# Clustered attention and a mixing MLP on one core: weighted values of a head pair in one run instead of two, with a new table of places

## The chip, the cores and the metric

The kernel runs on one core of a Trainium2 chip. The metric is the time of one execution on the device in microseconds. Before the change it is 1022.99 us, the median of two runs (1021.92 and 1024.06). One more execution was profiled.

## The reference

Attention over 4 batches, 8 heads, 768 positions and 64 dimensions, in which a query sees only keys of its own cluster, and after it a mixing layer and a multilayer stage, all in float32:

```
q_assign, k_assign = argmax over 16 centroids of the cosine with q and with k
mask    = q_assign[:, :, :, None] == k_assign[:, :, None, :]
scores  = where(mask, (q @ k.T) / 8, -1e9);  scores -= max(scores)
attn    = exp(scores) / (sum(exp(scores)) + 1e-9)
x       = (attn @ v), heads side by side                  # (4, 768, 512)
u       = x + ((x.T @ U) @ V).T                           # U: 768x32, V: 32x768
out     = u + relu(u @ w_ch1) @ w_ch2                     # 512 -> 2048 -> 512
```

## The kernel before, in words

**Stages.** Two heads are worked on together as a pair; there are 16 pairs, i = 0 to 15, four to a batch. After the attention of all pairs comes the multilayer stage (`gemm1`, `gemm2`, lines 600 to 624), which the change leaves alone.

**A pair.** `load` (L329) and `load_v` (L335) fetch queries and keys, and values, on the DMA queue of SyncE (SP). `sims` (L339) multiplies them with the centroids: four products into the four 32-column strips of the array, so narrow products. `largest` (L348) transposes the result, and DVE takes its maximum; `clusters` (L361) makes one-hot rows out of it, in place, in the same bank of PSUM. `clusters_T` and `place_clusters` bring these beside the keys, so that one product gives score and mask at once. `split_hi` (ACT) and `split_lo` (L390; DVE for one half, POOL for the other) make a high and a low part of queries and keys, and `place_keys_hi`, `place_keys_lo`, `place_queries`, `place_ones` copy parts of them on SP. `rowmax` (L445) makes a first score, 24 steps of one product and one reduction on DVE per pair; `rowmax_T` and `rowmax_place` bring the maxima back in as a row, by a DMA on ACT's queue. `scores` (L471) is run for 2 halves (h) times 6 blocks of keys (c): four products into one of two PSUM tiles `st`, and one exponential on ACT into a tile `pr`, of which there are 11. `weights` (L485) adds the exponentials of a half into a tile `T` (three buffers), mostly on POOL, five adds per half. `values` (L494) multiplies exponentials with values: per step two float32 products, one into the upper and one into the lower 64 columns of the array, each of them two instructions in the trace; six steps accumulate into one bank, which ACT then empties. `sums` (L506) multiplies the two T of a pair with a column of ones, four narrow products; `sums_T` and `normalise` finish the pair. After each batch `mix_u`, `mix_sum` and `mix_v` do the mixing layer.

All small PSUM tiles (`ps_max`, `ps_sim`, `ps_simT`, `o_ps`, `ps_sum`, ...) share the four work banks of `work` (L139). The weights of the multilayer stage arrive as float64 bits in between, joined to float32 by DVE and split in two parts by ACT and POOL (`load_weights`, L189).

**Order.** Each call is put on a list with a time (`at`, L639) and the list is sorted (L733); `keep_order` (L107) then keeps every engine to the order of the list. The times are in slots, 12 to a pair: `when(name, i)` is 12i plus an entry of the table `times` (L59), whose columns stand for kinds of pairs ("most", "last of a batch", "last", "first", "second", "third"). So each engine takes its instructions strictly in this order, and waits where one isn't ready.

The lines of the loop (L693 to L699) that place scores, values and adds; `GV` is 6, so values come in batches of six steps, 24 products as the trace counts them:

```
for k in range(NS):
    h, c = divmod(k, NT)
    at(when("scores", i) + k, scores, i, h, c)
    at(when("values", i) + GV * (k // GV) + GV - 1 + 0.001 * (k % GV), values, i, h, c)
    if c:
        at(when("weights", i) + k, weights, i, h, c)
at(when("sums", i), sums, i)
```

`GV` also groups the places of `rowmax` (L685), by the list `spots`.

Of the kernel before, what the change touches and what calls it, by code (L numbers as in the profile page):

```python
# [29 lines left out]
F32 = mybir.dt.float32  # L30
# [23 lines left out]
GV = 6  # L54
# [8 lines left out]
    "clusters_T":      (-19.46, -19.14,  -17.8,   None, -12.09, -13.37),  # L63
    "place_clusters":  (-18.22, -16.28, -15.03,   None, -10.34, -12.11),
    "split_hi0":       (-29.17, -30.74, -24.29,   None,   None, -21.38),
    "split_lo0":       (-24.05, -24.44, -24.04,   None,   None, -18.43),
    "split_hi1":       (-23.81, -23.71, -24.34,   None,   None, -19.53),
    "split_lo1":       (-23.67, -20.02, -23.57,   None,   None, -17.17),
    "place_keys_hi":   (-20.09, -23.61, -22.66,   None,   None, -17.07),
    "place_keys_lo":   (-19.84, -19.85,  -21.7,   None,   None, -16.87),  # L70
    "place_queries":   (-16.97, -16.19,  -16.3,   None,   None, -16.28),
    "place_ones":      (-14.55, -12.25,  -6.11,   None,   None, -20.84),
# [8 lines left out]
    "sums_T":          ( 16.16,  15.81,   14.3,  15.86,  17.06,  16.44),  # L81
    "normalise0":      ( 18.83,  16.88,  14.88,  19.57,  20.85,  21.01),
# [4 lines left out]


mixes = {
    "mix_u":    ( 18.88,  18.35,  18.48,  16.57),  # L90
    "mix_sum":  ( 19.11,   19.1,  19.15,  18.35),
    "mix_v":    (  20.5,   20.4,  20.68,  19.42),
}
# [671 lines left out]
```

## Time and profile before

| | |
|---|---|
| median of two runs | 1022.99 us |
| profiled execution, its own time | 1020.33 us |
| its span, first to last instruction | 1018.5 us |
| mean granted clock of TensorE | 0.993 |
| busy PE, DVE, POOL, ACT over the span | 97, 48, 35, 34% |
| first and last `values` product begin at | 42.1 and 461.0 us |

Engines are called PE (TensorE), DVE (VectorE), ACT (ScalarE), POOL (GpSimd) and SP (SyncE). A row of the timeline gives start and length in us, engine, line, operation, what it writes and reads, shape, and how many instructions were merged; in brackets the idle time of the engine before it and who ended it. Lengths of products overlap, so their pace is read from the starts. A row of groups gives the count behind x, then busy us and mean ns of one, and then the idle time before them. A row of stretches gives the length and the busy time of PE, weight loads, DVE, ACT and POOL, the granted clock, the share of DMA and GB/s.

### The profile page before, as it was taken

To read this page: it belongs to the slowest core of one execution; us is meant where nothing else is said; L and a number is where in the kernel's file an instruction comes from. 1 tells how busy PE (TensorE), PEld (TensorE's weight loads), DVE (VectorE), ACT (ScalarE), POOL (GpSimd) and SP (SyncE) were. 2 spreads that over 40 slices of the span, in tenths; PEclk is the share of its full clock that TensorE was granted. 3 is DMA by queue.
4 is the path that set the end of the run, shared out by engine and by line. 5 is a ranking of instruction groups with operands and counts; after the bars stand their busy time and mean duration, and the time that the engine had idled before them with its cause. 6 is when DMAs were issued, how large, how long until landed. Compare 5 with 4: busy or idle time off the path is not lost.

```text
span 1018.5 us, 13723 instructions
## 1 busy us (share of the span) xinstructions
PE 990.5 (97%) x5368; PEld 786.9 (77%) x5368; DVE 490.5 (48%) x914; ACT 347.7 (34%) x572; POOL 359.4 (35%) x246
## 2 busy tenths in 40 slices
PE   5899999999999999989999999999999999999998
PEld 3566666676667666657899999999999999998997
DVE  5797777777777666768772121121221211212211
ACT  4454554555556554564341111111111111111110
POOL 5466676888788967753230000000000000000000
PEclk9899999999999999999999999999999999999999
DMA  7754554656465636243431001010010010100000
GB/s 186 191 130 115 157 146 122 192 155 156 100 199 136 150 86 181 61 143 108 163 123 63 1 32 32 1 62 1 1 63 1 18 46 1 62 1 1 32 1 32
DMA packets 28687, 87.71 MB, mean 86 GB/s; under 512 B 4880, under 2 KB 9488, under 8 KB 28112
## 3 DMA queue, kind: packets, MB, share of 16 engines
q1 hardware_dynamic: 28240, 86.76, 30.5%
q8 instruction: 42, 0.69, 0.3%
q14 instruction: 21, 0.17, 0.1%
q10 hardware_dynamic: 384, 0.10, 0.0%
HBM read 42.99 MB, written 12.58 MB: 55 GB/s over the span
## 4 chain that ended last, share of the span: by engine, by line
PE 90%; DVE 5%; ACT 1%; issue 1%; POOL 1%; DMA 1%; ACTq 0%; SPq 0%; POOLq 0%; DVEq 0%
PE o_ps L500 12%; PE ps_h L606 9%; PE ps_h L608 9%; PE ps_h L607 9%; PE y L624 9%; PE y L623 9%; PE y L622 9%; PE ps_max L453 7%; PE st L477 6%; PE st L479 6%; DVE m L455 2%; PE ps_sum L512 1%; PE ps_sim L343 1%; PE ps_oT L533 1%; PE ps_uT L595 1%
## 5 line engine op out<-in xcount | busy, mean ns | idle before, releaser
L492 POOL TENSOR_TENSOR T<-T,pr 128x768 f32<-128x768 f32 x120 | 226.5, 1887 | 44.9 <-ACT pr L482 19.3
L612 DVE SCALAR_TENSOR_TENSOR hl<-ps_h,hh 128x384 fp32r<-128x384 f32 x128 | 71.2, 556 | 349.9 <-ACT hh L611 349.8
L455 DVE TENSOR_REDUCE m<-ps_max 128x1 f32<-128x384 f32 x384 | 195.2, 547 | 80.6 <-PE ps_max L453 79.0
L611 ACT ACTIVATE hh<-ps_h 128x384 fp32r<-128x384 f32 x128 | 62.9, 491 | 373.8 <-PE ps_h L608 373.8
L482 ACT ACTIVATE pr<-st 128x768 f32<-128x768 f32 x192 | 154.3, 812 | 83.5 <-PE st L479 65.4
L453 PE MATMUL ps_max<-arena 128*128 128x384 f32 x384 | 126.6, 380 | 6.9 <-DVE oh L369 2.5
L500 PE MATMUL o_ps<-pr,vt 128*64 128x384 f32 x768 | 132.2, 494 | 0.1
L623 PE MATMUL y<-w2l,hh 128*128 128x512 f32 x288 | 113.6, 395 | 0.0
L477 PE MATMUL st<-arena 128*128 128x384 f32 x384 | 104.9, 354 | 2.0 <-ACT pr L482 2.0
L453 PEld LDWEIGHTS ps_max<-arena 128*128 128x128 f32 x384 | 70.5, 192 | 45.4 <-issue 21.4
L500 PEld LDWEIGHTS o_ps<-pr,vt 128*64 128x64 f32 x768 | 52.7, 138 | 66.4 <-issue 59.8
L479 PE MATMUL st<-arena 97*128 97x384 f32 x384 | 99.2, 340 | 2.8 <-DMA arena<-mT 2.8
L477 PEld LDWEIGHTS st<-arena 128*128 128x128 f32 x384 | 66.2, 190 | 17.9 <-issue 9.3
L492 POOL TENSOR_TENSOR T<-pr 128x768 f32<-128x768 f32 x30 | 56.6, 1886 | 62.2 <-ACT pr L482 62.2
L624 PE MATMUL y<-w2h,hl 128*128 128x512 f32 x192 | 76.1, 396 | 0.0
L624 PE MATMUL y<-arena,hl 128*128 128x512 f32 x192 | 76.0, 396 | 0.0
L622 PE MATMUL y<-w2h,hh 128*128 128x512 f32 x192 | 75.1, 391 | 0.0
L622 PE MATMUL y<-arena,hh 128*128 128x512 f32 x192 | 74.8, 390 | 0.0
L479 PEld LDWEIGHTS st<-arena 97*128 97x128 f32 x384 | 70.4, 190 | 3.5 <-issue 2.2
L623 PEld LDWEIGHTS y<-w2l,hh 128*128 128x128 f32 x288 | 54.0, 188 | 9.1
L504 ACT COPY os<-o_ps 128x384 f32<-128x384 f32 x32 | 15.3, 480 | 104.7 <-PE o_ps L500 104.7
L606 PE MATMUL ps_h<-arena,w1h 128*128 128x384 f32 x128 | 44.8, 350 | 0.2 <-DVE arena L598 0.2
(132 smaller groups left out, 1597.3 us busy)
## 6 DMA issues: line engine op xcount, KB each, us to landing
rw<-in_w SPq DMA_DIRECT2D x32, 512.0 KB
R<-in_qk SPq DMA_DIRECT2D x32, 384.0 KB
arena<-arena SPq DMA_DIRECT2D x32, 384.0 KB
arena<-arena SPq DMA_DIRECT2D x64, 192.0 KB
vt<-in_v SPq DMA_DIRECT2D x16, 384.0 KB
u_scr<-xt SPq DMA_DIRECT2D x4, 1536.0 KB
u<-u_scr SPq DMA_DIRECT2D x8, 768.0 KB
out_y<-u SPq DMA_DIRECT2D x24, 256.0 KB
```

What stands on the lines that cost most here:

```text
L453: nc.tensor.matmul(ps[:, 0:HS], x1[:, 0, g // 2, g % 2, t * P:(t + 1) * P], x1[:, 1, h, g % 2, :], start=True, stop=True)
L455: nc.vector.reduce_max(live["m2", i][:, h, u:u + 1], ps[:, 0:HS], axis=AX.X)
L477: nc.tensor.matmul(st[:, j, 0:HS], x1[:, 1, hk, j, ks], x1[:, 0, h, j, :], start=True, stop=False)
L479: nc.tensor.matmul(st[:, j, 0:HS], x2[0:97, 1, hk, j, ks], x2[0:97, 0, h, j, :], start=False, stop=True)
L482: nc.scalar.activation(pr, st[:, :, 0:HS], AF.Exp, scale=SCALE)
L492: eng.tensor_add(T, live["p", i, h, 0] if c == 1 else T, live["p", i, h, c])
L500: nc.tensor.matmul(o_ps[64 * j:64 * j + 64, 0:HS], vv[:, c, j, :], pr[:, j, :], start=(c == 0), stop=(c == NT - 1))
L606: nc.tensor.matmul(ps[:, 0:HS], w1h[:, d, fs], uh[:, d, :], start=(d == 0), stop=False)
L607: nc.tensor.matmul(ps[:, 0:HS], w1h[:, d, fs], ul[:, d, :], start=False, stop=False)
L622: nc.tensor.matmul(y[t], hh[:, ts], w2h[:, f % FG, :], start=(f == 0), stop=False)
L623: nc.tensor.matmul(y[t], hh[:, ts], w2l[:, f % FG, :], start=False, stop=False)
L624: nc.tensor.matmul(y[t], hl[:, ts], w2h[:, f % FG, :], start=False, stop=(f == NF - 1))
```

## The change

`GV` becomes 12 and a new `GM` = 6 keeps the grouping of `rowmax`. So all 12 steps of a pair's values stand together, 48 products by the trace's count, and `sums` gets its place from them, half a slot after the last. `sims` of pair i now stands straight ahead of the values of pair i - 4, and `largest` of pair i straight ahead of the values of pair i - 3, wherever there is such a pair. There are 13 `pr` buffers instead of 11, two `vt` (values) instead of three, two `T` instead of three. Nearly all entries of `times`, `mixes`, `stages` and `spots` are new. No instruction is added or taken away.

Around the run of pair 6 the sorted list reads before (left) and after (right):

```
before, first half of the pair's values        after
  72.31  values (5, 1, 0..5)                     84.00  scores (7, 0, 0)
  ...                                            84.12  rowmax (8, 3, 1)
  78.31  values (6, 0, 0..5)                     84.41  split_lo (9, 0)
  ...                                            84.45  largest (9)
  84.12  rowmax (8, 3, 1)                        84.46  sims (10)
  84.31  values (6, 1, 0..5)                     84.47  values (6, 0..1, 0..5)
  84.61  rowmax (8, 4, 0)                        84.61  rowmax (8, 4, 0)
  84.95  largest (9)                             84.97  sums (6)
  86.31  sums (6)                                85.00  scores (7, 0, 1)
  86.70  clusters (9)                            85.60  clusters (9)
  94.90  sims (10)                               86.07  sums_T (6)
```

The diff, with the tables cut to the entries that the prediction speaks of:

```diff
--- before.py
+++ after.py
@@ -51,57 +51,58 @@
 NF = DF // P
 NG = 4
 FG = NF // NG
-GV = 6
+GV = 12
+GM = 6
 BIG = float(2.0 ** 60)
 SCALE = 0.125
 
 
 times = {
-    "load0":           (-34.78, -34.39, -43.85,   None,   None, -25.08),
-    "load1":           (-26.29, -29.07, -32.88,   None,   None, -24.23),
-    "sims":            ( -25.1, -28.59, -28.41,   None,   None, -21.52),
...
-    "place_clusters":  (-18.22, -16.28, -15.03,   None, -10.34, -12.11),
...
-    "split_lo0":       (-24.05, -24.44, -24.04,   None,   None, -18.43),
...
-    "load_v":          ( -19.2,  -5.08,  -7.21,   None, -22.04,  -9.26),
+    "load0":           ( -40.5,  -40.5,  -40.5,   None,   None,    -27),
+    "load1":           (-38.82,    -39, -38.79,   None,   None,  -25.5),
+    "sims":            (-24.38, -28.52, -28.41,   None,   None,  -24.5),
...
+    "place_clusters":  (-19.29,  -18.3,  -18.3,   None, -10.11, -13.71),
...
+    "split_lo0":       (-23.59, -24.44, -24.04,   None,   None, -20.27),
...
+    "load_v":          ( -8.39,  -8.42,   -8.5,   None,   -8.5,  -8.19),
...
-    "rowmax_T":        ( -3.08,  -3.31,  -3.73,  -3.18,   0.25,  -2.19),
-    "rowmax_place":    ( -2.26,  -2.27,   -2.6,   0.84,    2.2,  -0.15),
-    "scores":          (     0,  -0.97,  -0.37,  -0.47,   0.82,   0.95),
-    "weights":         (  1.45,  -0.22,   0.44,   2.06,   3.14,   1.67),
-    "values":          (  1.31,   1.51,   0.02,   1.05,   3.05,   1.39),
-    "sums":            ( 14.31,  14.69,  13.43,  14.01,  15.51,  15.47),
...
-    "largest":         (-23.05, -22.46, -20.21,   None,   None, -21.05),
-    "clusters":        ( -21.3, -22.24, -20.12,   None,   None, -18.18),
+    "rowmax_T":        ( -3.05,  -3.11,   -3.5,  -3.16,   0.25,  -2.19),
+    "rowmax_place":    ( -2.62,  -2.28,  -1.76,   0.84,    2.2,   -0.2),
+    "scores":          (  -0.1,      0,   0.69,   0.18,      0,      0),
+    "weights":         (  1.22,   1.79,    1.4,    1.4,    1.4,    1.4),
+    "values":          (  1.47,   1.57,   1.05,    1.5,   1.56,   1.48),
+    "sums":            ( 14.31,  13.43,  19.65,  13.87,  16.86,  16.13),
...
+    "largest":         (-23.92, -22.93,  -23.2,   None,   None, -21.05),
+    "clusters":        ( -22.4,  -22.4,  -22.4,   None,   None, -19.51),
 }
 
 
 mixes = {
-    "mix_u":    ( 18.88,  18.35,  18.48,  16.57),
...
+    "mix_u":    ( 16.36,   16.3,  15.82,   16.3),
...
 }
 
 
 stages = {
...
 }
 
-spots = [0.66, -0.06, 1.8, 2.25, 1.26, 2.09, 2.97, 3, 3.49, 3.81, 4.58, 5.03]
+spots = [0.54, -0.06, 1.8, 2.38, 1.26, 2.09, 2.87, 3, 3.49, 4.9, 4.58, 5.03]
 
 
 def keep_order(tc, first=0):
@@ -333,7 +334,7 @@
         nc.sync.dma_start(out=live["R", i][:, 2 * h:2 * h + 2], in_=qk[i // NP, i % NP, :, 2 * h:2 * h + 2])
 
     def load_v(i):
-        live["v", i] = sb.tile([P, NT, 2, D], F32, name="vt", bufs=3)
+        live["v", i] = sb.tile([P, NT, 2, D], F32, name="vt", bufs=2)
         nc.sync.dma_start(out=live["v", i], in_=v[i // NP, i % NP])
 
     def sims(i):
@@ -478,14 +479,14 @@
         for j in range(2):
             nc.tensor.matmul(st[:, j, 0:HS], x2[0:97, 1, hk, j, ks], x2[0:97, 0, h, j, :],
                              start=False, stop=True)
-        pr = sb.tile([P, 2, HS], F32, name="pr", bufs=11)
+        pr = sb.tile([P, 2, HS], F32, name="pr", bufs=13)
         nc.scalar.activation(pr, st[:, :, 0:HS], AF.Exp, scale=SCALE)
         live["p", i, h, c] = pr
 
     def weights(i, h, c):
 
         if c == 1:
-            live["T", i, h] = late.tile([P, 2, HS], F32, name="T", bufs=3)
+            live["T", i, h] = late.tile([P, 2, HS], F32, name="T", bufs=2)
         T = live["T", i, h]
 
         eng = nc.vector if (i, h, c) in {(0, 1, 1), (0, 1, 3), (15, 0, 1), (15, 0, 3), (15, 0, 5), (15, 1, 2), (15, 1, 3), (15, 1, 4), (2, 1, 2), (2, 1, 3)} else nc.gpsimd
@@ -670,7 +671,9 @@
             for h in range(2):
                 for fn in (load, split_hi, split_lo):
                     at(when(f"{fn.__name__}{h}", i), fn, i, h)
-            for fn in (sims, largest, clusters, place_keys_hi, place_keys_lo, place_queries, place_ones):
+            at(when("values", i - 4) + NS - 1.01 if i > 3 else when("sims", i), sims, i)
+            at(when("values", i - 3) + NS - 1.02 if i > 2 else when("largest", i), largest, i)
+            for fn in (clusters, place_keys_hi, place_keys_lo, place_queries, place_ones):
                 at(when(fn.__name__, i), fn, i)
         if i:
             for fn in (clusters_T, place_clusters, load_v):
@@ -682,8 +685,8 @@
                 if i < 3:
                     at(when("rowmax", i) + pace * u + 0.01 * h, rowmax, i, u, h)
                 else:
-                    g, r = divmod(2 * u + h, 2 * GV)
-                    at(when("rowmax", i) + GV * g + spots[r], rowmax, i, u, h)
+                    g, r = divmod(2 * u + h, 2 * GM)
+                    at(when("rowmax", i) + GM * g + spots[r], rowmax, i, u, h)
         if i == 1:
             at(when("rowmax_T", i) - 4, rowmax_T, i, 0, NT)
             at(when("rowmax_place", i) - 5, rowmax_place, i, 0, NT)
@@ -696,7 +699,7 @@
             at(when("values", i) + GV * (k // GV) + GV - 1 + 0.001 * (k % GV), values, i, h, c)
             if c:
                 at(when("weights", i) + k, weights, i, h, c)
-        at(when("sums", i), sums, i)
+        at(when("values", i) + NS - 0.5, sums, i)
         at(when("sums_T", i), sums_T, i)
         for h in range(2):
             at(when(f"normalise{h}", i), normalise, i, h)
```

More of the change, by code (lines that the diff above doesn't have):

```diff
@@ L59 @@
 times = {
-    "load0":           (-34.78, -34.39, -43.85,   None,   None, -25.08),
-    "load1":           (-26.29, -29.07, -32.88,   None,   None, -24.23),
-    "sims":            ( -25.1, -28.59, -28.41,   None,   None, -21.52),
-    "clusters_T":      (-19.46, -19.14,  -17.8,   None, -12.09, -13.37),
-    "place_clusters":  (-18.22, -16.28, -15.03,   None, -10.34, -12.11),
-    "split_hi0":       (-29.17, -30.74, -24.29,   None,   None, -21.38),
-    "split_lo0":       (-24.05, -24.44, -24.04,   None,   None, -18.43),
@@ L67 @@
[L67 to L72, printed above, removed]
-    "load_v":          ( -19.2,  -5.08,  -7.21,   None, -22.04,  -9.26),
@@ L81 @@
-    "sums_T":          ( 16.16,  15.81,   14.3,  15.86,  17.06,  16.44),
-    "normalise0":      ( 18.83,  16.88,  14.88,  19.57,  20.85,  21.01),
-    "normalise1":      ( 21.59,  17.72,  15.28,   26.3,  23.84,  20.15),
-    "largest":         (-23.05, -22.46, -20.21,   None,   None, -21.05),
-    "clusters":        ( -21.3, -22.24, -20.12,   None,   None, -18.18),
+    "load0":           ( -40.5,  -40.5,  -40.5,   None,   None,    -27),
+    "load1":           (-38.82,    -39, -38.79,   None,   None,  -25.5),
@@ new lines @@
+    "sims":            (-24.38, -28.52, -28.41,   None,   None,  -24.5),
+    "clusters_T":      (   -20,    -20,    -20,   None, -12.09, -14.65),
+    "place_clusters":  (-19.29,  -18.3,  -18.3,   None, -10.11, -13.71),
+    "split_hi0":       (-29.17, -30.74, -24.61,   None,   None, -21.68),
+    "split_lo0":       (-23.59, -24.44, -24.04,   None,   None, -20.27),
+    "split_hi1":       (-23.81, -23.76, -24.36,   None,   None, -18.89),
+    "split_lo1":       (-23.67, -21.02, -23.88,   None,   None, -17.76),
@@ new lines @@
+    "place_keys_hi":   (-20.09, -23.02, -22.66,   None,   None, -17.07),
+    "place_keys_lo":   (-19.72, -19.85, -22.38,   None,   None, -16.68),
+    "place_queries":   (-16.97, -18.07,  -16.3,   None,   None, -16.35),
+    "place_ones":      (-15.03, -12.61,  -6.11,   None,   None, -22.37),
+    "load_v":          ( -8.39,  -8.42,   -8.5,   None,   -8.5,  -8.19),
+    "rowmax":          (-14.88, -14.94,  -14.8, -12.52,  -8.11, -11.77),
+    "rowmax_T":        ( -3.05,  -3.11,   -3.5,  -3.16,   0.25,  -2.19),
@@ new lines @@
+    "rowmax_place":    ( -2.62,  -2.28,  -1.76,   0.84,    2.2,   -0.2),
[3 more added lines that the diff above has]
+    "sums":            ( 14.31,  13.43,  19.65,  13.87,  16.86,  16.13),
+    "sums_T":          ( 14.07,  14.07,  13.76,  13.86,  14.11,   13.8),
+    "normalise0":      ( 14.61,  14.56,  15.29,  14.92,  17.84,  14.75),
@@ L86 @@
+    "normalise1":      ( 16.78,  15.58,   15.6,  15.39,   15.6,  15.36),
+    "largest":         (-23.92, -22.93,  -23.2,   None,   None, -21.05),
+    "clusters":        ( -22.4,  -22.4,  -22.4,   None,   None, -19.51),
 }
 mixes = {
-    "mix_u":    ( 18.88,  18.35,  18.48,  16.57),
-    "mix_sum":  ( 19.11,   19.1,  19.15,  18.35),
-    "mix_v":    (  20.5,   20.4,  20.68,  19.42),
+    "mix_u":    ( 16.36,   16.3,  15.82,   16.3),
+    "mix_sum":  (  16.6,   16.6,  16.65,   16.6),
+    "mix_v":    ( 18.01,     18,  17.93,     18),
@@ L93 @@
 }
 stages = {
-    "mix":  (  3.36,   6.22,  11.43,  15.04,  15.04,  16.96),
-    "g0":   ( 35.66,  38.22,   42.3,  42.54,  42.54,  52.94),
-    "g1":   (-26.11, -21.73, -21.19,  -20.5,  -20.5, -18.29),
-    "g2":   ( -2.37,  -1.48,  -0.87,  -0.52,  -0.75,   0.36),
-    "g3":   (  5.26,   6.37,   6.46,   6.74,   7.45,   8.06),
+    "mix":  (  4.14,   6.41,   7.49,  15.61,  14.47,  17.12),
+    "g0":   ( 35.54,  38.92,   42.3,  39.86,  41.96,  53.07),
+    "g1":   (   -26, -21.87, -22.11,  -20.5, -20.97, -18.29),
@@ L102 @@
+    "g2":   (  -3.2,   -1.3,  -0.81,  -0.26,   -0.7,  -0.11),
+    "g3":   (  5.09,   6.42,   6.46,   7.58,   7.45,   8.06),
 }
-spots = [0.66, -0.06, 1.8, 2.25, 1.26, 2.09, 2.97, 3, 3.49, 3.81, 4.58, 5.03]
+spots = [0.54, -0.06, 1.8, 2.38, 1.26, 2.09, 2.87, 3, 3.49, 4.9, 4.58, 5.03]
 def keep_order(tc, first=0):
```

## The prediction

> **What bounds the kernel now.** I read the page first, its busy tenths in 40 slices: which engine is full, and where.
>
> ```profile
> PE   5899999999999999989999999999999999999998
> PEld 3566666676667666657899999999999999998997
> DVE  5797777777777666768772121121221211212211
> ```
>
> TensorE (PE) is full nearly throughout; VectorE (DVE) is close behind it in the first 18 slices, the attention, and far behind it afterwards, in the multilayer stage, which the change leaves alone. So I next read the busy time by stretches: the whole of the weighted values, and four head pairs (one batch) from its middle.
>
> ```profile
> 42.10:461.40 419.30, 408.88 (x2422) 272.80 (x2421) 317.45 (x609) 230.60 (x341) 316.15 (x172) 1.00 0.53 141
> ...
> 170.40:276.20 105.80, 105.67 (x641) 71.88 (x640) 81.12 (x160) 61.17 (x91) 87.79 (x49) 1.00 0.58 155
> ```
>
> The columns are the length, then busy PE, weight loads, DVE, ScalarE (ACT) and GpSimd (POOL). In the batch PE idles 0.13 us of 105.8. Divided by four, a pair takes 26.45 us, with DVE busy for 20.3 and POOL for 21.9. A pair thus costs what its products cost, and what the array loses between them. That loss shows in the timeline of PE around one run of 24 products and one group of similarities. Columns: start, length, and how many.
>
> ```profile
> 289.65 0.52 PE L453 MATMUL ps_max<-arena 128*128 128x384 f32 x2
> 290.10 4.09 PE L500 MATMUL o_ps<-pr,vt 128*64 128x384 f32 x24
> 294.12 0.45 PE L453 MATMUL ps_max<-arena 128*128 128x384 f32 x1
> 294.40 0.49 PE L533 MATMUL ps_oT<-ident,os 128*128 128x128 f32 x3
> ...
> 295.62 0.34 PE L453 MATMUL ps_max<-arena 128*128 128x384 f32 x1
> 295.80 0.51 PE L477 MATMUL st<-arena 128*128 128x384 f32 x2
> 296.15 0.51 PE L479 MATMUL st<-arena 97*128 97x384 f32 x2
> ...
> 299.05 0.52 PE L453 MATMUL ps_max<-arena 128*128 128x384 f32 x2
> 299.50 0.85 PE L343 MATMUL ps_sim<-R,cT 128*32 128x384 f32 x8
> 300.28 0.61 PE L477 MATMUL st<-arena 128*128 128x384 f32 x2
> 300.73 0.51 PE L479 MATMUL st<-arena 97*128 97x384 f32 x2
> ```
>
> Lengths overlap, so starts are compared. One row maximum (L453) takes 0.18 us when full-width work follows (295.62 to 295.80), so two take 0.35; ahead of the run two take 0.45 (289.65 to 290.10). Behind the run one takes 0.28 (294.12 to 294.40). So 0.10 is lost going in and 0.10 coming out. The run itself takes 4.02; cut in the middle, it shows its steady pace:
>
> ```profile
> 290.10 2.16 PE L500 MATMUL o_ps<-pr,vt 128*64 128x384 f32 x12
> ```
>
> Twelve more products lengthen it from 2.16 to 4.09, by 1.93, so 24 cost 3.86 inside a run, and another 0.16 goes at its ends. The similarities lose the same 0.10 on either side: 299.05 to 299.50 for two maxima, and 300.28 to 300.73 for two score products that otherwise take 0.35 (295.80 to 296.15).
>
> **The change, part by part.** Joined runs: each run that is joined to another saves 0.10 + 0.10 + 0.16 = 0.36 us. 32 runs become 16: 16 x 0.36 = 5.8 us less, all on PE, which sets the end of these stretches.
>
> Similarities: `sims` now stands straight ahead of a run. What the border between two narrow shapes costs is seen where `mix_u` follows a run:
>
> ```profile
> 260.59 4.09 PE L500 MATMUL o_ps<-pr,vt 128*64 128x384 f32 x24
> 264.61 1.91 PE L546 MATMUL ps_xu<-xt,u_w 128*32 128x512 f32 x12
> ```
>
> Again 4.02 from start to start, so the loss inside the run stays, and only the two times 0.10 beside it go. By the plan's times 12 groups move (pairs 4 to 15), and in one a row maximum still comes between: 11 x 0.20 = 2.2 us less. `mix_u` in turn leaves its run in three batches and stands alone: 3 x 0.20 = 0.6 more. The sums are not joined: in the sorted plan a row maximum, and in some pairs a score step too, lies between run and sums. Nothing for them.
>
> The Trainium skill (TensorEngine Tiling (Array Packing), Key Properties) says that a change of the tiling mode drains TensorE and a change of tile does not. By that rule a pair has eight changes of mode now and five afterwards; at half of 0.36 for each, the sum would be 16 x 3 x 0.18 = 8.6 us, where the rows give 7.4.
>
> So PE's own bill is 5.8 + 2.2 - 0.6 = 7.4 us lower. The rest is what may keep PE from collecting it.
>
> DVE. It lives on what PE gives it, and idles in a run once that is used up:
>
> ```profile
> 294.60 0.56 DVE L455 TENSOR_REDUCE m<-ps_max 128x1 f32<-128x384 f32 x1 [1.44 <-PE ps_max L453]
> ...
> 307.10 1.02 DVE L455 TENSOR_REDUCE m<-ps_max 128x1 f32<-128x384 f32 x2 [2.82 <-PE ps_max L453]
> 308.03 0.55 DVE L357 TENSOR_REDUCE mx<-ps_simT 128x24 f32<-128x384 f32 x1
> ...
> 309.09 1.01 DVE L455 TENSOR_REDUCE m<-ps_max 128x1 f32<-128x384 f32 x2
> ```
>
> It idled 1.44 us in one run of a pair, where it had a weight's bits to join, and 2.82 in the other. In the new plan it has for each run, in this order: up to two pending maxima (307.10 to 308.03: 0.93), one `split_lo`, and `largest` (308.03 to 309.09: 1.06). Next in its queue is the row maximum from behind the run, and behind that `clusters`, which needs nothing more of PE and yet waits.
>
> ```profile
> L393 DVE TENSOR_TENSOR arena<-R,arena 128x768 fp32r<-128x768 f32 x14 | 19.9, 1422 | 0.3 <-ACT arena L388 0.3
> ```
>
> That is 0.93 + 1.42 + 1.06 = 3.4 us of cover, or 2.5 when the maxima are done early. The run lasts 4.02 + 3.86 = 7.9 us, and the reduction behind it starts 0.5 after its end (294.12 to 294.60): 8.4. DVE will idle 5.0 to 5.9 in each run; I take 5.2, since an engine this full arrives with maxima pending. A pair then needs 20.3 + 5.2 = 25.5 us of DVE, and PE needs 26.45 - 7.4/16 = 26.0. PE stays the bound, by half a microsecond, too little for uneven pairs to pass without waits; `clusters` also keeps one of the four work banks in PSUM until it is done, so PE can run ahead by less. Bounds of these waits: nothing if the slack is used well; if DVE's other idle time (24.7/4 - 2.82 - 1.44 = 1.9 us a pair) stays as it is, 27.4 - 26.0 = 1.4 a pair. I take 0.2 a pair, near the lower end because that idle time follows PE's pace and not DVE's own. Over 11 middle pairs: +2.
>
> POOL. A pair's first add needs a T buffer, of which there are now two, so the sums of the pair before must have read theirs, and it needs the second exponential. Its last add must end before its own sums.
>
> ```profile
> L492 POOL TENSOR_TENSOR T<-T,pr 128x768 f32<-128x768 f32 x9 | 17.2, 1911 | 0.5
> L492 POOL TENSOR_TENSOR T<-pr 128x768 f32<-128x768 f32 x2 | 3.8, 1881 | 2.6 <-ACT pr L482 2.6
> L393 POOL TENSOR_TENSOR arena<-R,arena 128x768 fp32r<-128x768 f32 x1 | 1.8, 1811 | 0.0
> L205 POOL TENSOR_TENSOR w2l<-rw_t,w2h 128x512 fp32r<-128x512 f32 x1 | 1.3, 1281 | 0.0
> ```
>
> Ten adds at 1.9, one `split_lo` and one weight part are 22.1 us. Ahead of them come the sums (eight products like those of the similarities, 0.78), their 0.10, a score step (twice 0.35) and an exponential (0.8, quoted below): 2.4. Together 24.5 of 26.0: in the mean T is ready in time, and pairs without the channel mix, which are shorter than the mean, come close. Without that cover the sums wait, and behind them on PE all scores of the next pair. I count nothing, with 0 and 1 us a pair as the ends.
>
> Loads. The values have two buffers left: `load_v` of pair i stands at 12i - 8.4 slots, three slots after run i-2 (12i - 11.5) has freed the buffer, so the SP queue does not stop on it, and 21 slots before its use. Q and K are loaded some six slots earlier because `sims` is ten slots earlier; the last reader of their buffer stands seven slots before. The copies of keys and queries behind them on SP move by less than two slots. Nothing, between 0 and the 1.9 us that one late copy costs in the row of 435.76 below.
>
> The 13th exponential buffer lets one score step of the next pair go ahead of the run: no added work, only 0.8 us of ACT and the first wait of POOL earlier.
>
> The end of the attention has waits of its own, which the new order moves:
>
> ```profile
> 433.24 0.61 PE L477 MATMUL st<-arena 128*128 128x384 f32 x2 [1.46 <-ACT pr L482]
> 435.76 0.87 PE L479 MATMUL st<-arena 97*128 97x384 f32 x2 [1.91 <-DMA arena<-mT]
> 436.57 5.42 PE L500 MATMUL o_ps<-pr,vt 128*64 128x384 f32 x24
> ```
>
> ```profile
> L482 ACT ACTIVATE pr<-st 128x768 f32<-128x768 f32 x12 | 9.3, 818 | 1.0 <-PE st L479 1.0
> L204 ACT CAST arena<-rw_t 128x512 fp32r<-128x512 f32 x5 | 3.2, 633 | 0.0
> L159 ACT ACTIVATE rw_g<-rw 128x512 f32<-128x512 f32 x3 | 2.1, 691 | 0.2 <-DMA rw<-in_w 0.2
> ```
>
> The three PE rows hold 1.46 + 1.91 + (5.42 - 4.09) = 4.7 us of waiting. The DMA of the last row maxima now has run 14 (7.9 us) between itself and the first score of pair 15: that 1.91 goes. But the last two pairs no longer have a run among their scores. After run 14 ACT has 9.3 + 3.2 + 2.1 = 14.6 us to do (groups of 436.6 to 461.4), against 12 x 0.70 = 8.4 of scores and some 3 of sums and transposes on PE; about 3 us of that would show as a wait, less what ACT still owes when run 15 begins. Between -4.7 and +3 I take -2. The start keeps its list, and pairs 0 to 2 only change places: 0, within 3 either way.
>
> **Sum.** -7.4 + 2 - 2 = -7.4. The profiled execution took 1020.33 us (span 1018.5 and 1.8 around it), so 1013 by its own measure. The median of the two runs, 1022.99, lies 2.7 higher, which would make it 1015.6; between the two I say **1014.5**, 0.8% below the median. About 2% is what a measurement of this kernel tells from no change.
>
> **Rivals.** (1) DVE takes PE's place: the idle time of the long run comes on top of what DVE idles anyway, 20.3 + 5.2 + 1.9 = 27.4 us a pair against 26.45 now. Over 11 pairs that is +10, less 2 at the end: 1029 to 1033, slower than before. It decides as soon as the maxima behind a run cannot catch up before the next. For it: DVE's row of 7s on the page, and `clusters` queued on the wrong side. Against: most of the 1.9 us is DVE waiting for PE, which it then would not. The Trainium skill (TensorEngine Tiling (Array Packing), PSUM Bottleneck) warns that tiling speeds TensorE but not what empties PSUM, which would make it this rival; 20.3 us of DVE against 26.45 of PE say not yet.
>
> (2) POOL is late: should each add take a tenth longer, 24.5 becomes 26.4 us a pair, the sums wait, and nothing is gained: 1019 to 1022. For it: 22.1 us of work that now must fit between sums and sums. Against: batches with a longer, mixing pair let it catch up.
>
> (3) The new places remove more waits than I count: 7.4, all 4.7 at the end and 2 in the first pairs, none added: 1006 to 1009. For it: PE idles 419.3 - 408.9 = 10.4 us in the whole stretch. Against: ACT's backlog at the end.
>
> (4) The change does not do what it says, since the array pauses inside the long run for reasons of its own: 1020 to 1023. The even pace of the cut run speaks against it.
>
> **How the numbers follow.** My forecast 0.48, DVE 0.18, POOL 0.14, more removed 0.14, nothing saved 0.03, several engines late together and beyond 1043 0.03. The forecast alone spans 1008 to 1020. The range takes in rival 1 nearly to its end and most of rival 3: 1004 to 1032. Faster by over 2% means below 1002.5, beyond rival 3: 0.05. Slower by over 2% (above 1043): 0.04. Within: 0.91.
>
> **What would show it.** Right: 16 runs of 48 products in 7.9 us each, PE idle under 1 us a pair between them, DVE waiting about 5 us for the maximum behind each run, no wait for T at the sums. DVE wrong: PE waits over 1 us a pair for `m` (L455). POOL wrong: PE waits for T. End wrong: PE waits over 5 us for `pr` behind run 14. The forecast fails altogether if a middle pair takes over 26.5 us or under 25.4 in the mean.

## The result and the profile after

The changed kernel takes 1077.18 us, the median of two runs (1075.21 and 1079.16), against 1022.99 (1021.92 and 1024.06): 5.3% slower, ratio 1.0533 (95% interval 1.0494 to 1.0573). 1014.5 was predicted, and the range ended at 1032. The page of the kernel after, with the rows that answer to those shown of before:

```profile
span 1073.4 us, 13732 instructions
PE 1004.8 (94%) x5368; PEld 794.1 (74%) x5368; DVE 478.8 (45%) x914; ACT 349.3 (33%) x572; POOL 359.8 (34%) x246
PE   5888989988998999887999999999999999999998
DVE  6657666765677767667465112122121221211211
...
L456 DVE TENSOR_REDUCE m<-ps_max 128x1 f32<-128x384 f32 x384 | 193.5, 547 | 131.5 <-PE ps_max L454 129.4
L480 PE MATMUL st<-arena 97*128 97x384 f32 x384 | 102.3, 348 | 19.0 <-DMA arena<-mT 19.0
```

PE was at 9 in nearly all slices of the attention; now about every second one is an 8. Two groups have changed. DVE idles 131.5 us ahead of the reductions of row maxima (80.6 before), which was foreseen in kind. PE idles 19.0 us ahead of the second half of the scores (2.8 before), which was not: it waits for the DMA that brings the row maxima in. PE's own row is a surprise too: the same 5368 products, and 1004.8 us of them instead of 990.5. By stretches (from the seventh exponential of the first pair, which in the kernel before falls together with the first values product, to the end of the last values product; one batch; then what follows the attention; columns as before):

```profile
47.70:517.60 469.90, 421.55 (x2435) 280.19 (x2437) 316.39 (x612) 233.02 (x346) 316.13 (x173) 0.97 0.47 125
191.66:315.41 123.75, 111.83 (x641) 73.68 (x641) 81.74 (x160) 61.17 (x90) 88.27 (x49) 0.96 0.50 133
518.20:1073.40 555.20, 550.60 (x2805) 495.25 (x2801) 132.97 (x236) 96.05 (x190) 23.32 (x16) 1.00 0.11 37
```

The multilayer stage takes 555.2 us, as before, so everything is lost ahead of it. A batch takes 123.75 us instead of 105.80: PE idles 11.9 us in it instead of 0.1, is busy 6.2 us longer, and its granted clock is 0.96 instead of 1.00; DVE, ACT and POOL do the same work as before. The timeline of PE around one run of the middle shows both losses.

```profile
243.90 0.27 PE L466 MATMUL ps_mT<-ident,m 128*12 128x128 f32 x1
...
246.29 0.54 PE L478 MATMUL st<-arena 128*128 128x384 f32 x2
249.10 0.92 PE L480 MATMUL st<-arena 97*128 97x384 f32 x2 [2.28 <-DMA arena<-mT]
249.82 0.52 PE L454 MATMUL ps_max<-arena 128*128 128x384 f32 x1
250.14 0.84 PE L354 MATMUL ps_simT<-ident,sims 128*128 128x128 f32 x3
250.91 1.51 PE L344 MATMUL ps_sim<-R,cT 128*32 128x384 f32 x8
252.35 8.05 PE L501 MATMUL o_ps<-pr,vt 128*64 128x384 f32 x48
260.33 0.44 PE L454 MATMUL ps_max<-arena 128*128 128x384 f32 x1
```

The pair's first score stands ahead of the run and needs the row maxima in its second half (L480). PE takes its list in order, so it stands still for 2.28 us with 48 products ready behind. After that the work is slow: the similarities span 1.51 us instead of 0.85. The same place in the rows of ACT's queue and of SP's:

```profile
244.21 0.27 ACT L468 ACTIVATE mT<-ps_mT 12x128 fp32r<-12x128 f32 x1
244.51 0.73 ACTq L230 DMA_DIRECT2D arena<-mT  x1
```

```profile
241.97 0.58 SPq L334 DMA_DIRECT2D R<-in_qk  x1
242.59 0.80 SPq L230 DMA_DIRECT2D arena<-ones  x1
243.44 0.50 SPq L334 DMA_DIRECT2D R<-in_qk  x1
243.98 0.43 SPq L152 DMA_DIRECT2D rw<-in_w  x1
```

The small DMA is issued at 244.51, and PE goes on at 249.10: 4.59 us. Two loads of queries and keys (384 KB each) and one of weights (512 KB) were issued in the 2.6 us ahead of it. In the kernel before the same step, for another pair of the middle, was:

```profile
298.84 0.73 ACTq L229 DMA_DIRECT2D arena<-mT  x1
```

```profile
299.50 0.85 PE L343 MATMUL ps_sim<-R,cT 128*32 128x384 f32 x8
...
301.43 0.52 PE L477 MATMUL st<-arena 128*128 128x384 f32 x2
301.80 0.51 PE L479 MATMUL st<-arena 97*128 97x384 f32 x2
```

There the score could begin 2.96 us after the issue, without a wait; the similarities, moved away by the change, filled 0.78 us of that time, and the loads had been issued 2.3 us and more ahead. Not all of the 19.0 us is time that the DMA took: the longest of the ten waits, 4.09 us that ended at 95.87, was for a DMA issued at 93.89, so there the row maxima themselves were late.

The slow work has its own rows. The record of the granted clock changes only at steps of 3.41 us; here are four pairs of neighbouring steps in the kernel after (the granted clock is the third number from the end):

```profile
215.04:218.45 3.41, 1.55 (x9) 1.09 (x8) 1.78 (x4) 1.50 (x2) 3.25 (x3) 1.00 0.60 203
218.45:221.86 3.41, 3.41 (x17) 1.75 (x17) 2.34 (x3) 1.53 (x2) 3.25 (x3) 0.50 0.00 0
245.76:249.17 3.41, 1.13 (x7) 0.77 (x6) 1.95 (x4) 1.10 (x2) 3.25 (x3) 1.00 0.55 209
249.17:252.58 3.41, 3.41 (x16) 1.75 (x18) 2.10 (x4) 1.62 (x3) 3.33 (x2) 0.50 0.00 0
337.92:341.33 3.41, 2.35 (x14) 1.97 (x12) 2.69 (x6) 1.63 (x2) 3.33 (x2) 1.00 0.94 344
341.33:344.74 3.41, 2.62 (x19) 1.53 (x21) 1.78 (x3) 1.90 (x3) 3.25 (x3) 1.00 0.01 2
447.15:450.56 3.41, 1.80 (x11) 1.44 (x10) 1.62 (x4) 1.80 (x3) 3.33 (x3) 1.00 0.88 194
450.56:453.97 3.41, 2.29 (x13) 1.91 (x12) 2.64 (x6) 1.52 (x2) 3.25 (x3) 1.00 0.71 266
```

Where PE idled 1.86 or 2.28 us of one step (3.41 less 1.55 or 1.13), the next step ran at half the clock; where it idled 1.06 or 1.61, not. The wait of 1.85 us that ended at 342.12 cost no clock: the border at 341.33 cut it in two, 1.06 and 0.79 us, and no half-clock step followed. Behind the half-clock start of the program there are seven half-clock stretches of 3.41 us and one of 6.83 at the end, against one of 3.41 in the kernel before: 27.3 us more. (That start lasted 10.24 us before and 13.65 after, but that isn't the edit's doing: the kernel below with the similarities at the run begins with the list of before and had 13.65.) Products of that time take about twice as long, so up to 13.7 us more, an estimate: nearly all of PE's 14.3 us of added busy time, as its list of products is the same.

### The profile page after: what moved, and what is told of

It reads as the page before. It is cut to its first block, busy times and chain, and to the rows that moved or that the text cites. A ratio compares the mean times of both kernels' runs of the same rounds, so it can differ in the third digit from the quotient of the medians.

```text
span 1073.4 us, 13732 instructions
## 1 busy us (share of the span) xinstructions
PE 1004.8 (94%) x5368; PEld 794.1 (74%) x5368; DVE 478.8 (45%) x914; ACT 349.3 (33%) x572; POOL 359.8 (34%) x246
## 4 chain that ended last, share of the span: by engine, by line
PE 80%; DVE 6%; DMA 6%; ACT 3%; issue 2%; SPq 1%; POOL 1%; ACTq 0%; DVEq 0%; POOLq 0%
PE o_ps L501 12%; PE ps_h L607 8%; PE ps_h L609 8%; PE ps_h L608 8%; PE y L625 8%; PE y L624 8%; PE y L623 8%; PE ps_max L454 4%; PE st L480 4%; DMA arena<-mT 3%; PE st L478 3%; DVE m L456 3%; ACT pr L483 1%; PE ps_sim L344 1%; DMA arena<-arena 1%
## 5 line engine op out<-in xcount | busy, mean ns | idle before, releaser
L456 DVE TENSOR_REDUCE m<-ps_max 128x1 f32<-128x384 f32 x384 | 193.5, 547 | 131.5 <-PE ps_max L454 129.4
L493 POOL TENSOR_TENSOR T<-T,pr 128x768 f32<-128x768 f32 x120 | 226.3, 1886 | 21.8 <-DVE T L493 11.1
L501 PE MATMUL o_ps<-pr,vt 128*64 128x384 f32 x768 | 128.8, 492 | 3.9 <-DVE arena L599 2.0
L480 PE MATMUL st<-arena 97*128 97x384 f32 x384 | 102.3, 348 | 19.0 <-DMA arena<-mT 19.0
L454 PEld LDWEIGHTS ps_max<-arena 128*128 128x128 f32 x384 | 73.0, 196 | 58.9 <-issue 18.7
L480 PEld LDWEIGHTS st<-arena 97*128 97x128 f32 x384 | 71.6, 194 | 22.2 <-DMA arena<-mT 14.8
```

The costliest lines, as they stand in the source:

```text
L454: nc.tensor.matmul(ps[:, 0:HS], x1[:, 0, g // 2, g % 2, t * P:(t + 1) * P], x1[:, 1, h, g % 2, :], start=True, stop=True)
L456: nc.vector.reduce_max(live["m2", i][:, h, u:u + 1], ps[:, 0:HS], axis=AX.X)
L480: nc.tensor.matmul(st[:, j, 0:HS], x2[0:97, 1, hk, j, ks], x2[0:97, 0, h, j, :], start=False, stop=True)
L493: eng.tensor_add(T, live["p", i, h, 0] if c == 1 else T, live["p", i, h, c])
L501: nc.tensor.matmul(o_ps[64 * j:64 * j + 64, 0:HS], vv[:, c, j, :], pr[:, j, :], start=(c == 0), stop=(c == NT - 1))
```

## The experiments

Three theories stood at the beginning. **A**: the first score ahead of the long run waits for the DMA of the row maxima, and the half clock behind it doubles the price. **B** (rival 1 of the prediction): DVE idles through each long run and cannot make that up, so PE waits for it or for the PSUM banks that it keeps. **C**: the values' load, which now holds SP's queue until a run has ended, pushes the loads behind it to the moment of that DMA. The edits are against the kernel after unless said otherwise; ratios are to the kernel before on the same chip. The table shows when the seventh of a pair's twelve exponentials, the first of its second half, begins (timeline of ACT in each profile, in us), so that start, middle and end are seen apart. It is chosen because at that point every kernel has the values of the pair before behind it and none of this pair's; "pair 4 begins" below means this point. Pair 0 lies between 46.5 and 48.8 in the kernels with all new places, whose half-clock start lasted 10.24 to 20.48 us, so differences of 1 or 2 us between two profiles say little.

| kernel | median | ratio, 95% interval | pair 0 | pair 4 | pair 8 | pair 12 |
|---|---|---|---|---|---|---|
| before | 1022.99 | | 42.2 | 154.6 | 260.6 | 366.2 |
| after | 1077.18 | 1.0533 (1.0494 to 1.0573) | 47.8 | 180.1 | 303.9 | 417.1 |
| first score behind | 1061.10 | 1.0379 (1.0363 to 1.0396) | 48.1 | 176.9 | 291.3 | 403.0 |
| and long run from pair 4 only | 1055.85 | 1.0343 (1.0308 to 1.0378) | 46.5 | 169.1 | 282.6 | 394.6 |
| two runs, new places | 1047.07 | 1.0245 (1.0223 to 1.0267) | 48.2 | 167.7 | 280.3 | 390.4 |
| long run, old places | 1074.24 | 1.0506 (1.0490 to 1.0522) | 42.4 | 169.5 | 295.2 | 417.5 |
| old plan, new start | 1029.17 | 1.0064 (1.0040 to 1.0089) | 45.6 | 161.6 | 268.7 | 374.2 |
| old plan, similarities at the run | 1026.50 | 1.0043 (1.0031 to 1.0055) | 42.2 | 155.8 | 264.3 | 371.4 |
| values loaded last | 1097.14 | 1.0732 (1.0718 to 1.0746) | 46.7 | 186.1 | 316.0 | 434.5 |

**The first score behind the run.** One line of the loop; beside it the same with three buffers for values (`vt`, bufs=3) and 12 for exponentials (`pr`, bufs=12), so that SP isn't held.

```diff
-    at(when("scores", i) + k, scores, i, h, c)
+    at(when("values", i - 1) + NS - 0.95 if i and not k else when("scores", i) + k, scores, i, h, c)
```

> The changed kernel, but the first score step of every pair stands behind the long run instead of ahead of it. Theory A (the step ahead of the run waits for the DMA that brings in its row maxima; TensorE idles 19 us so, and each wait of about 2 us is followed by 3.4 us at half clock): the waits for mT fall from 19 to under 3 us, the seven half-clock stretches of the attention to two or fewer, and the time from 1077 to 1045-1052. Theory B (the long run starves VectorE, which idles 7.9 us in each and cannot catch up): TensorE waits for VectorE's row maxima instead, 1065-1077. Theory C (the load of the values, with two buffers, holds the SP queue until the run ends, so that large loads crowd the small DMAs): some gain, 1060-1070, waits for other DMAs stay.

> The first score step behind the run as in e1, 12 exponential buffers (the 13th has no use then) and three buffers for the values again, so that the SP queue does not stop for the run. Theory A: the same as e1 within 3 us. Theory C: 5 to 15 us faster than e1, and the SP queue's 150 us of waiting for TensorE at the load of the values gone. Theory B: as e1.

Measured: 1061.10 us, 16 less than the kernel after, and 1062.33 with the third buffer, which is the same. No wait for the row maxima is left (19.0 us before this edit), nor any half-clock stretch from 130 to 485 us. So A holds, for 16 of the 54 us, where its range (1045 to 1052) asked for 25 and more; the rest is elsewhere, and the hold of SP by itself is not it. From pair 4 to pair 12 the edit saves 10.9 us: 8.1 of PE's idle time, and 2.8 of its busy time, with three half-clock stretches there before it and none behind it.

**Loads issued earlier.** The loads of queries and keys from pair 6 on, and the first weight loads, go ahead of the values' load.

```diff
-    at(when(f"{fn.__name__}{h}", i), fn, i, h)
+    at(NS * i - 44.9 + 0.1 * h if fn is load and i > 5 else when(f"{fn.__name__}{h}", i), fn, i, h)
-    "g0":   ( 35.54,
+    "g0":   ( 27.04,
```

> The changed kernel, with the loads of queries and keys and of the weights' bits issued ahead of the load of the values, so that they run during the long run and not beside the DMA of the row maxima. Nothing else moves. Theory A with a flight time that the crowd sets (issue to arrival 4.2-4.7 us where TensorE waits, under 3 us before the change): waits for mT fall from 19 to about 6 us, time 1050-1060. Theory A with a flight time of its own: 19 us stay, 1075-1080. Theory C: as the first, 1050-1060. Theory B: 1075-1080.

Measured: 1083.26 us (1.0599, 1.0572 to 1.0625), slower than after. From PE's timeline and its table of waits:

```profile
246.39 0.54 PE L478 MATMUL st<-arena 128*128 128x384 f32 x2
247.28 0.59 PE L480 MATMUL st<-arena 97*128 97x384 f32 x2 [0.35 <-DMA arena<-mT]
```

```profile
PE ps_max L454 <- DMA arena<-arena: 11.9, 3, 5.3
PE st L480 <- DMA arena<-mT: 8.9, 4, 5.4
PE ps_max L454 <- DMA arena<-ones: 7.6, 2, 4.0
```

The part about the DMA came true: issued at 244.61, with no load of queries and keys beside it, it was through by 247.28, in 2.67 us instead of 4.59, and PE waited 0.35. The time didn't follow, since now the copies of keys stand behind the loads on SP, which wait 110.2 us for DVE's and POOL's `split_lo` (none of it in the kernel after), and row maxima wait 19.5 us for the copies.

**The values' load last.** It is put behind the other loads of its time, so that it holds nothing.

```diff
-    for fn in (clusters_T, place_clusters, load_v):
+    for fn in (clusters_T, place_clusters):
         at(when(fn.__name__, i), fn, i)
+    at(NS * i - 0.3 if i > 2 else when("load_v", i), load_v, i)
```

> The changed kernel with one edit: from pair 3 on the load of the values stands eight slots later in the list, behind the loads of queries, keys and weights, so that the SP queue does not stop for the long run. The first score stays ahead of the run. Theory C (SP is held until the run ends, and the large loads then fly beside the DMA of the row maxima, which takes 4.2-4.7 us in place of 2.4-2.7): waits for mT in pairs 4 to 12 fall from 2 us each to under 0.6, at least three of the seven half-clock stretches go, 1077 becomes 1055-1065. Theory A without a crowd: 1073-1080.

Measured: 1097.14 us, 20 more than after. The SP queue, and what PE then did:

```profile
250.18 0.59 SPq L334 DMA_DIRECT2D R<-in_qk  x1
250.82 0.80 SPq L230 DMA_DIRECT2D arena<-ones  x1
251.66 0.49 SPq L334 DMA_DIRECT2D R<-in_qk  x1
252.21 0.42 SPq L152 DMA_DIRECT2D rw<-in_w  x1
252.73 0.37 SPq L338 DMA_DIRECT2D vt<-in_v  x1
```

```profile
258.90 1.01 PE L480 MATMUL st<-arena 97*128 97x384 f32 x2 [3.47 <-DMA arena<-mT]
```

The row maxima's DMA was issued at 253.12, so it took 5.79 us with four large loads ahead of it. C as it was put falls: SP is then held by a copy that waits for ACT's one-hot rows (96.3 us of such waits over the profile, 21.2 in the kernel after), and the load that was to be out of the way joined the crowd. The crowd itself is what counts for the DMA: for this pair it took 2.67 us with one large load issued shortly ahead, a weight's, 4.59 with three, 5.79 with four.

**Two runs on the new places.** `GV` is set back to 6; all new places and buffers stay.

```diff
-GV = 12
+GV = 6
```

> The changed kernel with its new table of places, its buffers and its first score ahead, but with the values in two runs of 24 again (the first half of a pair six slots earlier). Theory B: VectorE's long idle stretches are gone, 1035-1055. Theory A: the first score still stands ahead of the DMA, so the waits for mT stay within 5 us of 19 and the time is 1070-1085 (5.8 us of run ends come back).

Measured: 1047.07 us. The long run costs 30 us on these places, and the new places and buffers cost 24 without it. B's range holds and A's doesn't, but that is not B's proof: the edit shifts the loads against the DMA as well. In this trace no R load is issued in the 3.5 us ahead of the row maxima's DMA from pair 3 on, and PE waits for that DMA once, 1.5 us. What PE waits for from pair 4 to pair 12 (167.7 to 390.4 us), where it idles 9.5 us of 222.7 instead of 0.3 of 211.6:

```profile
PE ps_max L454 <- ACT ohT L381: 4.0, 5, 1.1
PE o_ps L501 <- DVE m L456: 2.4, 2, 1.2
PE ps_mT L466 <- DVE m L461: 2.0, 6, 0.5
```

The row maxima's DMA isn't among them.

**The long run on the old places.** The kernel before with one run per pair and the new buffers (13 `pr`, two `vt`, two `T`) and places of the values' load.

```diff
-    at(when("values", i) + GV * (k // GV) + GV - 1 + 0.001 * (k % GV), values, i, h, c)
+    at(max(when("scores", i) + 11.5, when("scores", i + 1) - 0.1 if i < n - 1 else when("values", i) + 11) + 0.001 * k, values, i, h, c)
```

> The kernel before, with its old table of places, and only the long run put in: a pair's 48 products straight ahead of the next pair's first score where that is possible (in last pairs of a batch one score step stays ahead), with 13 exponential, two values and two T buffers and the new places of the load of the values. Theory B (the long run starves VectorE): it loses by itself, 1.0-1.9 us a pair against 26.45, 1035-1050. Theory D (the loss lies in the new places and not in the run): the run ends save 5.8 us and nothing waits, 1012-1022.

Measured: 1074.24 us, 52 more than before, beyond what either theory gave. A batch takes 125.7 us; in it PE waits 4.0 us once for a load (`R`), 2.9 for POOL's sums `T`, 2.9 for DVE's weight bits, and runs at 0.97 of the clock. So the old places don't suit this kernel either. How much of the 52 is the long run's own stays open, because the buffers changed with it: SP waits 130.1 us at the values' load (3.7 before).

**The start's places alone.** In the kernel before, the columns "first", "second" and "third" and the loads of the mixing weights take their new values; a line of the 26:

```diff
-    "load0":           (-34.78, -34.39, -43.85,   None,   None, -25.08),
+    "load0": (-34.78, -34.39, -43.85, None, None, -27),
...
```

> The kernel before (short runs, old buffers), but with the new places for pairs 0, 1 and 2 and for the mixing weights; the other pairs keep their old places. In the changed kernel with two runs, pair 4 begins 13 us later than before. Theory D: the new start costs most of that by itself, 1030-1038. If the loss came from the later pairs' new places instead: 1020-1026.

Measured: 1029.17 us, just below D's range; pair 4 begins 7.0 us later, and little is added after that (8.0 at pair 12).

**Cover for DVE in the run.** First the one-hot rows, with the first score behind the run:

```diff
+    at(when("values", i - 3) + NS - 1.005 if i > 2 else when("clusters", i), clusters, i)
```

> The first score behind the run as in e1 (1061 us), and the three VectorE operations of clusters (1.7 us) queued ahead of the row maximum that follows the run, so that they are done while the run lasts. Theory B: VectorE idles 1.7 us less in each run and a middle pair gets 1-1.7 us shorter, 1040-1050. Theory D: no change, 1058-1064.

Then also the joins of the weights' bits:

```diff
-    "g0":   ( 35.54,  38.92,   42.3,  39.86,  41.96,  53.07),
+    "g0":   ( 31.54,  34.92,   42.3,  36.47,  36.47,  53.07),
```

> As e8, and the joining of a weight's bits on VectorE (2.2 us a pair in pairs 2 to 9) also queued into the run, with its load and its ScalarE step earlier. Theory B: 1-2 us less in each of the eight pairs, 8-16 us faster than e8. Theory D: within 3 us of e8.

And the first of the two with the values' load last, by the edit shown for it above:

> The long run with all that helped or should: first score behind it, clusters queued into it (e8, 1059 us) and the load of the values last. Theory C beyond the waits for mT: copies of keys and loads of queries wait less, 1048-1055. If the SP queue no longer matters once the first score is behind the run: 1056-1061.

Measured: 1058.70 (1.0345, 1.0323 to 1.0367), 1059.88 (1.0370, 1.0343 to 1.0398) and 1060.19 (1.0370, 1.0356 to 1.0384): the best is 2.4 us below the first score behind alone (1061.10, ratio 1.0379), where B gave 11 and more. In the first, DVE makes the one-hot rows during the run; it idles 5.0 us per run of pairs 4 to 13 in the mean instead of 6.9, and yet a middle batch takes 113.8 us, against 114.4. In the second the wait for `ohT` is gone from the batch, and PE waits 2.4 us for copies on SP instead. So B falls as a matter of DVE's total: giving DVE more to do in the run gained next to nothing. The third lies where the SP queue no longer matters.

**Similarities alone, and with the sums.** In the kernel before, `sims` goes straight ahead of a run; in a second kernel the sums of nine pairs as well.

```diff
+    at(when("values", i - 3) + 2 * GV - 1.001 if i > 4 else when("sims", i), sims, i)
```

```diff
+    late_sums = 2 < i < n - 2 and i % NP < NP - 1
-    at(when("sums", i), sums, i)
+    at(when("values", i + 1) + GV - 1.001 if late_sums else when("sums", i), sums, i)
...
```

> The kernel before, with short runs and its old places, but sims straight ahead of the second run of a pair from pair 5 on, where it stood 1.6 slots earlier: only the border between full-width and narrow products is saved. By the prediction's price of 0.20 us each, 11 x 0.20 = 2.2 us less: 1019-1021 beside 1022. If every displaced step costs a wait, as in the new table of places: 1022-1028.

> As e11, and the sums of nine pairs straight ahead of the first run of the next pair, with the steps that follow them up to four slots later. Another 9 x 0.20 = 1.8 us less by the price of the border: 1017-1020. If the later sums and normalising steps meet the row maxima on VectorE: 1021-1028.

Measured: 1026.50 and 1029.08 us (1.0065, 1.0047 to 1.0083), slower by 0.4 and 0.7% instead of faster by 0.2 and 0.4%; the second lies above both of its ranges. The table of PE's waits in the first shows it:

```profile
PE st L479 <- DMA arena<-mT: 5.5, 7, 1.9
```

Seven waits for the row maxima, two before the edit: part of the time that this DMA needed had been the similarities. It is not the whole loss. From pair 4 to pair 12 this kernel takes 4.0 us more than before, and 1.6 of these are waits for the DMA.

**The long run from pair 4 on, and one place put back.** Both with the first score behind the run. In the second, `clusters_T` and `place_clusters` of the middle pairs are back at -19.46 and -18.22. Its edit leaves the long run in all pairs, other than its expectation says, so the kernel beside it is the one with the first score behind (1061.10).

```diff
-    at(when("values", i) + GV * (k // GV) + GV - 1 + 0.001 * (k % GV), values, i, h, c)
+    at(when("values", i) + (GM * (k // GM) + GM if i < 4 else NS) - 1 + 0.001 * (k % GM if i < 4 else k), values, i, h, c)
```

```diff
-    "clusters_T":      (   -20,
+    "clusters_T":      (-19.46,
-    "place_clusters":  (-19.29,
+    "place_clusters":  (-18.22,
```

> First score behind the run as in the first experiment, but pairs 0 to 3 have their values in two runs of 24 products; from pair 4 on one run of 48. If the long run hurts at the start, where the first pairs still wait for their own inputs, and hardly in the middle, pair 4 begins where the new places with short runs have it (167.7 us, against 176.9 with long runs throughout), the middle stays as it was (pair 4 to pair 12 in 226 us), and the time is about 1052, against 1061. If the first score behind the run is what costs the start its 9 us, pair 4 still begins near 177 and the time stays at 1061.

> The kernel with the long run from pair 4 on, and the transposition of the one-hot rows with its copy back at the places of before (-19.46 and -18.22 slots in place of -20 and -19.29) for the middle pairs. In the middle batch PE waited three times about 1 us for the bank that ACT's copy of these rows holds. If that is a price of this one place, a batch gets some 3 us shorter (113 to 111) and the time falls by 7 to 10 from the kernel beside it. If the time moves by under 2 us, the wait goes to the next tile in line and no single place holds it.

Measured: 1055.85 us, and pair 4 begins at 169.1: the start's share belongs to the long run. The second gave 1.0366 (1.0339 to 1.0394), against 1.0379: 1057.81 to 1062.47 us, where the kernel beside it had 1059.49 to 1061.68. So this one place has no price by itself; which waits took over isn't shown.

No version was faster than the kernel before.

## Why the prediction was wrong

The saving on PE's own work came as forecast; what failed is what was put at nothing or near it: the new places (24 us), the first score behind a DMA among crowded loads (16), and what the long run costs beside its saving (14 lost where 5.8 were to be gained).

**Joined runs: right.** Where the clock was full:

```profile
344.14 7.96 PE L501 MATMUL o_ps<-pr,vt 128*64 128x384 f32 x48
352.03 0.44 PE L454 MATMUL ps_max<-arena 128*128 128x384 f32 x1
```

48 products in 7.89 us, and so in 12 of the 16 runs; 7.9 was predicted. The saving of 0.16 us inside each joined run is real: the values of a batch take 32.17 us before (eight runs) and 31.57 with the first score behind (four), 0.6 less. It is small beside what follows.

**DVE in the run: right in kind, both sizes too small.** The rows of DVE behind two runs:

```profile
260.81 0.56 DVE L456 TENSOR_REDUCE m<-ps_max 128x1 f32<-128x384 f32 x1 [7.87 <-PE ps_max L454]
...
352.51 0.56 DVE L456 TENSOR_REDUCE m<-ps_max 128x1 f32<-128x384 f32 x1 [5.26 <-PE ps_max L454]
```

5.26 us is the least and 7.87 the most in pairs 4 to 13; the mean is 6.5, and 6.9 with the first score behind, against 5.2 of the prediction (5.0 to 5.9). So DVE mostly did not arrive with maxima pending. And 0.2 us a pair for PE's waits on DVE was too little. With the first score behind, PE waits so in a middle batch (188.4 to 302.8 us):

```profile
PE ps_max L454 <- ACT ohT L381: 2.5, 3, 1.1
PE o_ps L501 <- DVE m L456: 0.9, 1, 0.9
PE ps_mT L466 <- DVE m L461: 0.9, 2, 0.6
```

With two more of 0.2 us on DVE that makes 2.2 us, 0.55 a pair. The upper bound that the prediction named was 1.4.

**Loads and the first score: a step that failed, 16 us.** "Nothing, between 0 and the 1.9 us that one late copy costs": the prediction asked whether each load comes in time for its own reader, and SP for its own queue. Its answer for SP was wrong: the queue does stop on the values' load, 150.0 us in 12 waits that end with a run, since SP runs ahead of the list's times and reaches the load before the buffer is free. That by itself cost nothing that the runs show: with the first score behind, a third buffer left the time as it was. And it didn't ask what else is in flight. The loads came out just ahead of the row maxima's DMA, which then took 4.2 to 4.7 us where 2.3 stood between its issue and its reader. The row of 435.76, quoted in the prediction for the end alone, was a wait of this kind (1.91 us, 4.26 after its issue, a weight load issued 0.1 us behind that, and one half-clock stretch). The sentence on the 13th buffer, "no added work", is the same gap: the step ahead of the run adds no work, but it made 48 ready products wait. Taking the score out of that place gave back 16 us.

**The new places at nothing, and with them the middle's 26.0 us per pair: the step that cost most, 24 us.** The prediction took for granted that PE would go on idling next to nothing (0.13 us in a batch of before). With short runs on the new places, one batch takes 112.6 us instead of 105.8, and pair 4 to pair 12 takes 11.1 us more. PE's idle time there is 9.2 us more, spread over the waits shown above: for ACT's copy of the one-hot rows, 4.0 us, and for DVE's maxima, 4.4. That is read from the waits, and no experiment removes the loss: with long runs, the one-hot rows' old places gained nothing, and where the joins' new places took this wait away, others came. Nor are places and buffers told apart in the 24. "2.2 us less" for the similarities had the wrong sign where it was tried, on the old places (4.0 us more from pair 4 to pair 12); on the new ones with short runs PE doesn't wait for the row maxima's DMA there, so this is not a part of the 11.1.

**The start, "0, within 3 either way": wrong.** Pair 4 begins 25.5 us later than before. The kernels in a row give the parts, in this order of edits: 7.0 for the new start columns alone (161.6 less 154.6), 6.1 more with all new places (167.7), 1.4 with the first score behind the run (169.1), 7.8 with long runs in the first pairs (176.9), 3.2 with the first score ahead of them (180.1). Of the 7.8, 1.6 are there at pair 0 already, before any long run. From there to pair 4, the kernel with long runs throughout has one wait of 4.0 us for SP's copy of the one-hot rows (1.0 with short runs), 1.9 for other copies (none with short runs), and three half-clock stretches instead of one.

**The end, -2: wrong sign.**

```profile
500.38 1.01 PE L478 MATMUL st<-arena 128*128 128x384 f32 x2 [4.32 <-ACT pr L483]
```

ACT's backlog behind run 14, foreseen at 3 us, is 4.32, and the half clock sets in during it, from 498.34 to 505.17. From pair 12 to the multilayer stage the kernel after loses 4.2 us.

**The rivals.** POOL isn't late in the kernel after: no sum waits for T. On the old places it is (5.9 us over the profile). DVE as the bound is what the longer idle time in the run speaks for, but its price was 6 to 10 us of the 54, and more cover for DVE gained 2.4 us at best.

The medians sum it up: 24 us for the new places and buffers with two runs, 9 for the long run from pair 4 on with the score behind it (6 in the profiled executions, in place of a gain of 12 x 0.36 = 4), 5 for long runs at the start (the intervals of these two kernels overlap, the start of pair 4 shows it), 16 for the first score ahead of the run. The 16 are shown by the edit that takes them away. Why the new places and the long run cost what they do is known by waits alone and stays open as a cause. How much of the 16 the half clock alone makes was not tried.

What the Trainium skill states of the clock (TensorE: Matmul & The Clock Gate, What's actually happening) is a free-running window of 3413 ns, and half rate after at least one idle window. The rows agree on the window: the clock changed only at steps of 3.41 us. They disagree on the amount: 1.86 us of idle time within one window was enough here.

## What to carry to other kernels

In a kernel whose order is written by hand and whose bound engine idles 0.1% of the time, price a move by what each neighbour was covering, not by its own work: here 0.8 us of similarities was part of the time that a small DMA needed. For every step ahead of a long run, write down when its last operand is issued, what large loads are issued beside it, and how long the run behind it would stand. A wait of some 2 us on TensorE is to be counted with the half clock behind it, here 3.41 us at half speed.

## What the runs showed of the hardware that was not expected

- The small DMA of row maxima (12 x 128 numbers, ACT's queue) depends on the large loads issued just ahead of it on SP's. Its last packet ended 1.5 to 1.8 us after the issue in pairs 2 to 14 of the kernel before, where no large load was issued in the 2 us ahead. It ended after 3.65 to 4.09 us in six pairs of the kernel after (3, 4, 6, 7, 8, 10), with two loads of queries and keys and one of weights in the 3.1 us ahead, and the waiting product began 4.2 to 4.7 us after the issue; with the values' load as a fourth it began after 5.8 to 6.5 (4.6 once, where the loads were spread over 3.4 us). With two loads issued 2.9 and 1.5 us ahead and none later (pair 11) it ended after 1.52 us in the kernel after and 2.27 in the one with the first score behind.
- The granted clock changes at steps of 3.41 us only, and half-clock steps follow steps in which PE idled much. In the kernel after, idle time of 1.86 us and more in one step was followed by a half-clock step, and 1.61 and less wasn't. The border isn't sharp: in the kernel with the first score behind the run, one half-clock step followed 1.12 us of idle time while 1.54 had none behind it, and in the one with the long run from pair 4 on, one followed 1.48.
